# Experts as a chain of whole blocks with branch hints and one shared section for left-over tokens

## The chip, the cores and the metric

The kernel runs on one core of one Trainium2 chip. The metric is the device time of one execution in microseconds (us), as a median of runs. The engines are named as in the profile: PE (TensorE, matmuls; PEld its weight loads), DVE (VectorE), ACT (ScalarE), POOL (GpSimd) and SP (SyncE, which here only issues DMAs). Each engine has its own instruction stream, with its own copies of every branch; engines wait for each other by semaphores.

## The reference, cut to what matters

```python
x = attention(u, v, z)                 # (8*3072, 256) rows, squared-ReLU attention, times u
do_compute = x @ w_skip > 0            # about half of the rows
e_idx = argmax(x[do_compute] @ w_gate) # one of E = 8 experts for each such row
for e in range(8):                     # D = 256, F = 1024
    h = np.maximum(xc[mask] @ w1[e], 0.0)
    y[mask] = gate_w[mask, None] * (h @ w2[e])
out[do_compute] = xc + y
x = out
h = maximum(maximum(x @ m1, x @ m2), x @ m3)   # 256 -> 768, all 24576 rows
result = h @ m_out
```

How many rows an expert gets is known only on the chip. With the inputs that are timed, worked out from the reference, the eight experts get 1381, 1685, 1697, 1770, 1589, 1311, 1337 and 1665 rows.

## The kernel before

Everything is fp32, split into a high and a low part (float32r), and each product is three matmuls (high by high, low by high, high by low). The work has three stages: attention with routing, the experts, and the last layer (its three up-projections with a maximum, here called the max weights, and a down-projection).

Routing scatters each row, with its gate value and its row number, into a region of the DRAM tensor `xb` that belongs to its expert; skipped rows go straight to their place in the result part of `xb`. A table `tab` in SBUF holds the count of each expert and the row offset of each block of it. The last block's offset is set back so that a block of 512 never reaches beyond the expert's rows; rows that are computed twice give the same result twice.

An expert's rows are worked off in blocks of T = 512 rows. `block(e, s, k, o, side)` has eight steps f: `mm1` (L637 on) makes one 128-wide piece of the hidden layer with six matmuls of 512 columns into one of four PSUM buffers `ph`, ACT makes `h_hi` (L646) and DVE `h_lo` (L647); two steps later `mm2` (L651) multiplies that piece with w2, twelve matmuls of 256 columns into `y`. At the end `finish` (L663) lets DVE add the gated result to the rows `xr` (L667, one instruction for each 128 rows), and POOL scatters them (L90). `o` leaves out the first 0, 128 or 256 of the 512 rows, so the block's end comes in three sizes: 512, 384 and 256 rows. `k` picks the buffers `xr`, `ids` and half of `yb`. The dictionary `side` holds work that is written in front of a step: splitting the next expert's weights (`split_w`), transposing and splitting the next block's rows (`split_x`, from the raw rows `xq`), or loads on SP.

`body(e)` (L883) is the block that every expert is taken to have (block 0; of expert 0 block 1, since block 0 is done early, within the attention's end). It is straight code and carries most of the side work. `chain(e, n_e, j)` (L849) follows with tests at run time: is there a block j at all (L852), is it a full one (L863), and in the `Else` (L874) has it more than 256 rows. A full one calls `chain` for j + 1 inside itself, up to j = 6, where a loop takes over. So the code of the tails lies behind that of all deeper full blocks. With the counts above, expert 0 has body and a tail of 384 rows; experts 1, 2, 3, 4 and 7 have body, two full blocks and a tail of 256; experts 5 and 6 have body, one full block and a tail of 384.

At the end the order is another: the bodies of experts 6 and 7 follow each other, then come the chain of 6 and that of 7, with the first loads of the last layer between them (`load2`, `trans2`). The max weights and the down weights lie split in DRAM and are loaded in one go in the body of expert 1 (four DMAs of 1.5 MB).

The instruction order is written out by hand (`manual_schedule`), engine by engine in the order of the code. Where a branch joins, the framework brings the semaphores of both ways to the same count: the way that skips work waits for its own engine's last count and adds what the other way would have added.

Of the kernel before, what the change touches and what calls it, by code (L numbers as in the profile page):

```python
# [17 lines left out]
SP = mybir.EngineType.SP  # L18

# [7 lines left out]
def attention_moe_kernel(  # L27
# [43 lines left out]
    tab = const.tile([1, SNAP + 1], I32, name="tab")  # L71
# [63 lines left out]
    with ExitStack() as st:  # L135
# [459 lines left out]
        ids = [const.tile([P, TB, 1], I32, name=f"ids{k}") for k in range(2)]  # L595
# [9 lines left out]
        def load_x(src, q, n):  # L605
            why = "results go to rows before those of the experts"
            if q is not None:
                for i in load_blocks(nc.sync, xq[q], src[:, 0:D]):
                    tc.declare_no_dep(i, group="out", reason=why)
            if n is not None:  # L610
                i = nc.sync.dma_start(xr[n], src.rearrange("(n p) w -> p n w", p=P)).ins
                tc.declare_no_dep(i, group=f"out{1 - n}", reason=why)
# [9 lines left out]
        def split_x(q, s, h, eng=nc.vector):  # L622
            xt = xt1[0][:, h * T:(h + 1) * T]
            hi, lo = xT[s][0, h], xT[s][1, h]
            nc.vector.transpose(out=xt, in_=xq[q][h])
            split(hi, lo, xt, eng)
# [10 lines left out]
        def mm1(e, s, o, f, p):  # L637
            hi, lo = (t[:, o:] for t in hT[f % 4])
            c, p = f * P % T, p[:, o:]
            terms = [(h, i, m) for h in range(DH) for i, m in ((0, 0), (0, 1), (1, 0))]  # L640
            for k, (h, i, m) in enumerate(terms):
                nc.tensor.matmul(  # L642
                    p, e1[e % 2][i, h, f * P // T][:, c:c + P], xT[s][m, h][:, o:],
                    start=k == 0, stop=k == len(terms) - 1,
                )
# [5 lines left out]
        def mm2(e, k, o, f):  # L651
            b, hh = e2[e % 2][f], hT[f % 4]
            started = set()
            for n in range(o // P, TB):
                y, c = yb[2 * k + n // 2], slice(n * P, (n + 1) * P)
                for i, m in ((0, 0), (0, 1), (1, 0)):
                    nc.tensor.matmul(  # L657
                        y[:, n % 2], hh[i][:, c], b[:, m],
# [4 lines left out]
        def finish(k, o):  # L663
            x, ix = xr[k], ids[k]
            nc.vector.tensor_copy(ix, x[:, :, D + 1:D + 2])
            for n in range(o // P, TB):
                nc.vector.scalar_tensor_tensor(  # L667
                    x[:, n, 0:D], in0=yb[2 * k + n // 2][:, n % 2], scalar=x[:, n, D:D + 1], in1=x[:, n, 0:D],
                    op0=ALU.mult, op1=ALU.add,
                )  # L670
            scatter_rows(x, ix, range(o // P, TB), "out", f"out{k}")

        def block(e, s, k, o, side):
            for f in range(NF):
                for g in side.get(f, ()):
                    g()
                mm1(e, s, o, f, ph[f % len(ph)])
                if f > 1:
                    mm2(e, k, o, f - 2)
            for g in side.get(NF, ()):  # L680
                g()
            mm2(e, k, o, NF - 2)
            mm2(e, k, o, NF - 1)
            finish(k, o)
# [118 lines left out]
        block(0, 0, 0, 0, side)  # L803
        ph.append(bank_tile("pm", [P, T], "ph"))
        xt1.append(slab("ut", [P, DH * T], name="xt"))
        pieces = [slab(tag, dt=F32R, name="w") for tag in ("hh",) * 2 + ("ll",) * 2 + ("hl",) * 6]
# [5 lines left out]
        xT.append({(m, h): slab("a", dt=F32R, name="xT") for m in range(2) for h in range(DH)})  # L812
        for _ in weights:
            pass
# [8 lines left out]
        def spread(a):  # L823
# [7 lines left out]
        nc.vector.tensor_tensor(first, thr, spread(cnt), op=ALU.is_lt)  # L831
        nblk = r_p.tile([1, E], F32, name="nblk")
        nc.vector.tensor_reduce(nblk, first, axis=AX.X, op=ALU.add)
        nc.vector.tensor_copy(tab[:, E:2 * E], nblk)
        nc.vector.scalar_tensor_tensor(
            tab[:, SNAP:], in0=snap, scalar=float(2 * T), in1=cnt[:, 0:1], op0=ALU.is_ge, op1=ALU.mult
# [9 lines left out]
    def tokens_of(e):  # L846
        return nc.values_load(tab[0:1, e:e + 1], min_val=0, max_val=N)

    def chain(e, n_e, j, other=None):  # L849
        if j == NT:  # L850
            return
        with tc.If(n_e > j * T) as some:  # L852
            if j == NJ:
                n_b = nc.values_load(tab[0:1, E + e:E + e + 1], min_val=0, max_val=NT)
                with tc.For_i(NJ, n_b) as i:
                    with tc.manual_schedule():
# [3 lines left out]
                        block(e, 1, 0, 0, {})  # L860
                return
            s, k = 0 if (e, j) == (E - 1, 1) else 1 + (j - 1) % 2, j % 2
            with tc.If(n_e > j * T + 3 * P) as full:  # L863
                with tc.manual_schedule():
                    side = {}
                    if j + 1 < NJ:
                        src = source(e, j + 1)
                        load_x(src, 0, None)
                        load_x(src, None, 1 - k)
                        side = {5 + h: [do(split_x, 0, 1 + j % 2, h)] for h in range(DH)}  # L870
                    block(e, s, k, 0, side)
                chain(e, n_e, j + 1)
# [7 lines left out]
        if other is not None:  # L880
            with some.Else():
                other()
# [3 lines left out]
    def body(e):  # L886
        j0 = 1 if e == 0 else 0
        n_e = tokens_of(e) if e else None
        with tc.manual_schedule():
            side = {f: [] for f in range(NF + 1)}  # L890
            src = source(e, j0 + 1)
            load_x(src, 0, None)
            if e + 1 < E:
                if e != E - 2:
                    load_x(source(e + 1, 0), 1, None)
# [140 lines left out]
```

## Time and profile before

| | us |
|---|---|
| median of 3 runs (4335.49 to 4337.26) | 4336.86 |
| the profiled execution | 4339.29 |
| its span, first to last instruction | 4337.6 |
| PE busy in it | 4214.1 (97%) |
| experts, from the end of expert 0's body to the last layer's first matmul | 622.8 |

Times below are from the start of the span. A PE matmul's row is longer than the time until the next one starts, since they are pipelined: the pace is read from the distances between starts. "Idle before" is the time in which the engine did nothing before that instruction, and the arrow names what ended it; "issue" is an end that no semaphore explains. Branch instructions have no row of their own.

### The profile page before, as it was taken

To read this page: it belongs to the slowest core of one execution; us is meant where nothing else is said; L and a number is where in the kernel's file an instruction comes from. 1 tells how busy PE (TensorE), PEld (TensorE's weight loads), DVE (VectorE), ACT (ScalarE), POOL (GpSimd) and SP (SyncE) were. 2 spreads that over 40 slices of the span, in tenths; PEclk is the share of its full clock that TensorE was granted. 3 is DMA by queue.
4 is the path that set the end of the run, shared out by engine and by line. 5 is a ranking of instruction groups with operands and counts; after the bars stand their busy time and mean duration, and the time that the engine had idled before them with its cause. 6 is when DMAs were issued, how large, how long until landed. Compare 5 with 4: busy or idle time off the path is not lost.

```text
span 4337.6 us, 63208 instructions
## 1 busy us (share of the span) xinstructions
PE 4214.1 (97%) x22380; PEld 3609.0 (83%) x22380; DVE 2824.4 (65%) x5641; ACT 2160.0 (50%) x4048; POOL 403.8 (9%) x677
## 2 busy tenths in 40 slices
PE   7999999999999999999989899999999999999999
PEld 6888888888888888888888888888888888888887
DVE  6888888888888888887544454444444444444444
ACT  6777686877768687775322232222222222222222
POOL 2111110011111001003111112000000000000000
PEclk9999999999999999999999999999999999999999
DMA  7787868678786867877453432111111111111110
GB/s 191 188 200 188 188 184 195 175 197 196 192 186 181 206 178 194 197 187 171 129 135 86 94 93 66 33 30 35 34 30 30 32 37 30 30 30 40 30 30 25
DMA packets 849941, 506.30 MB, mean 117 GB/s; under 512 B 446850, under 2 KB 807810, under 8 KB 834146
## 3 DMA queue, kind: packets, MB, share of 16 engines
q1 hardware_dynamic: 832738, 455.58, 44.8%
q0 software_dynamic: 15712, 45.28, 3.2%
q8 instruction: 212, 3.47, 0.4%
q14 instruction: 223, 1.83, 0.1%
q10 hardware_dynamic: 1056, 0.13, 0.0%
HBM read 274.19 MB, written 202.03 MB: 110 GB/s over the span
## 4 chain that ended last, share of the span: by engine, by line
PE 89%; DMA 3%; DVE 2%; issue 2%; ACT 2%; SPq 1%; POOL 0%; DVEq 0%; ACTq 0%
PE ph L958 28%; PE acc L308 21%; PE acc L309 11%; PE ph L642 7%; PE y L657 6%; PE y L971 6%; PE s L241 3%; PE s L242 3%; PE y L972 3%; DMA xb<-xr,ids 1%; PE pm L354 1%; DVE alo L276 1%; DMA back<-mirror 1%; DMA vr<-in_v 1%; ACT ahi L275 1%
## 5 line engine op out<-in xcount | busy, mean ns | idle before, releaser
L308 PE MATMUL acc<-vt,ahi 128*128 128x512 f32 x4608 | 1649.6, 396 | 7.1 <-DVE x L325 3.3
L309 PE MATMUL acc<-vt,alo 128*128 128x256 f32 x4608 | 1292.6, 281 | 0.1
L958 PE MATMUL ph<-e,mw 128*128 128x512 f32 x5184 | 1249.9, 394 | 3.4 <-DMA xb<-xr,ids 3.4
L958 PEld LDWEIGHTS ph<-e,mw 128*128 128x128 f32 x5184 | 955.8, 188 | 219.2 <-issue 3.5
L308 PEld LDWEIGHTS acc<-vt,ahi 128*128 128x128 f32 x4608 | 868.4, 188 | 210.9 <-DVE x L325 4.9
L309 PEld LDWEIGHTS acc<-vt,alo 128*128 128x128 f32 x4608 | 872.8, 189 | 30.5 <-DVE alo L276 1.5
L619 ACT ACTIVATE h_hi<-r 128x512 fp32r<-128x512 f32 x288 | 182.0, 632 | 782.1 <-DVE r L963 782.1
L276 DVE TENSOR_TENSOR alo<-a,ahi 128x512 fp32r<-128x512 f32 x672 | 460.5, 685 | 147.2 <-ACT ahi L275 136.8
L247 ACT ACTIVATE a<-s 128x512 f32<-128x512 f32 x672 | 398.1, 592 | 192.2 <-PE s L242 169.4
L962 DVE TENSOR_TENSOR r<-ph,r 128x512 f32<-128x512 f32 x288 | 199.2, 692 | 376.2 <-PE ph L958 376.0
L275 ACT ACTIVATE ahi<-a 128x512 fp32r<-128x512 f32 x672 | 411.8, 618 | 11.1 <-DVE a L253 10.8
L971 PE MATMUL y<-mo,h_hi 128*128 128x512 f32 x1152 | 417.1, 394 | 0.0
L90 POOL DMA_INDIRECT xb<-x,idx x192 | 212.2, 1105 | 1752.1 <-DVE alo L276 1044.2
L276 DVE TENSOR_TENSOR alo<-back,ahi 128x512 fp32r<-128x512 f32 x480 | 329.9, 692 | 55.8 <-ACT ahi L275 46.1
L275 ACT ACTIVATE ahi<-back 128x512 fp32r<-128x512 f32 x480 | 289.0, 625 | 146.2 <-PE acc L308 96.4
L282 DVE STREAM_TRANSPOSE turned<-a 128x512 f32<-128x512 f32 x480 | 338.4, 705 | 13.3 <-DMA mirror<-turned 13.3
L620 DVE TENSOR_TENSOR h_lo<-r,h_hi 128x512 fp32r<-128x512 f32 x288 | 199.5, 693 | 201.1 <-ACT h_hi L619 201.1
L647 DVE SCALAR_TENSOR_TENSOR h_lo<-ph,h_hi 128x512 fp32r<-128x512 f32 (+2 forms) x232 | 146.3, 631 | 276.5 <-ACT h_hi L646 264.7
L972 PE MATMUL y<-mo,h_lo 128*128 128x256 f32 x1152 | 325.4, 282 | 0.2 <-DVE h_lo L620 0.2
L963 DVE TENSOR_TENSOR r<-ph,r 128x512 f32<-128x512 f32 x288 | 199.2, 692 | 182.0 <-PE ph L958 182.0
L646 ACT ACTIVATE h_hi<-ph 128x512 fp32r<-128x512 f32 (+2 forms) x232 | 127.5, 549 | 378.7 <-PE ph L642 341.1
L241 PE MATMUL s<-hh,hl 128*128 128x512 f32 x672 | 271.8, 405 | 36.4 <-ACT a L247 22.4
(129 smaller groups left out, 4984.3 us busy)
## 6 DMA issues: line engine op xcount, KB each, us to landing
mirror<-turned SPq DMA_DIRECT2D x120, 1024.0 KB
back<-mirror SPq DMA_DIRECT2D x480, 256.0 KB
xq<-xb SPq DMA_DIRECT2D x608, 64.0 KB
vr<-in_v SPq DMA_DIRECT2D x48, 512.0 KB
ut<-in_u SPq DMA_DIRECT2D x48, 512.0 KB
out<-r SPq DMA_DIRECT2D x47, 512.0 KB
r<-in_moe_w SPq DMA_DIRECT2D x16, 1024.0 KB
xr<-xb SPq DMA_DIRECT2D x29, 528.0 KB
```

What stands on the lines that cost most here:

```text
L241: nc.tensor.matmul(s, w, hh, start=True, stop=False)
L247: nc.scalar.activation(a, s, AF.Relu)
L275: nc.scalar.activation(hi, a, AF.Copy)
L276: nc.vector.tensor_tensor(lo, a, hi.bitcast(F32), op=ALU.subtract)
L282: nc.vector.transpose(out=turned[0][:, :, n], in_=a.rearrange("k (c j) -> k c j", j=Q))
L308: nc.tensor.matmul(o, hn, vv, start=kb == 0, stop=False, skip_group_check=True)
L309: nc.tensor.matmul(o[:, 0], ln, vv[:, 0], start=False, stop=kb == KB - 1, skip_group_check=True)
L642: nc.tensor.matmul(p, e1[e % 2][i, h, f * P // T][:, c:c + P], xT[s][m, h][:, o:], start=k == 0, stop=k == len(terms) - 1,)
L657: nc.tensor.matmul(y[:, n % 2], hh[i][:, c], b[:, m], start=f == 0 and n // 2 not in started, stop=f == NF - 1 and i == 1, skip_group_chec ...
L958: nc.tensor.matmul(p, w[:, h, s, c], xT2(i, m, h), start=k == 0, stop=k == len(terms) - 1)
L971: nc.tensor.matmul(yb[n], hh[0][:, c], mo[:, f], start=f == 0, stop=False, skip_group_check=True)
L972: nc.tensor.matmul(yb[n][:, 0], hh[1][:, c], mo[:, f, 0], start=False, stop=f == NFF - 1, skip_group_check=True)
```

## The change

1. `chain` keeps only whole blocks: one test for each block, whether more than 384 rows of it are there, no `Else`. A full block hints the branch of the next one at step 3.
2. What is left over (at most 384 rows) is worked off after the chain in `rest`: a block of the last 256 rows, and if more than 256 are left a second one of 128 rows (`first=1, end=2`). It has buffers of its own: `xr` and `ids` number 2, the split rows `xT[3]`, raw rows `xq[2]` over the router weights `wgs`; the results use the `yb` of k = 0, swapped (`result`).
3. These rows (384 of them) are loaded at the end of the expert before, and split in the body at steps 1 and 2. For expert 0 they are loaded and split in its own body, at steps 6 and 7, and the weight splits there move to earlier steps.
4. Hints: `foresee` writes on all five engines an instruction that computes the branch's condition and hands it to the instruction fetch as a hint for a named branch.
5. Six small DVE operations make the left-over counts; `body` loads two numbers of the table in place of one.
6. Experts 6 and 7 now come in the same order as the others; `trans2` stands between expert 7's chain and its `rest`.
7. The max weights are loaded in four parts, at the ends of the bodies of experts 1 to 4.

```diff
-        def mm1(e, s, o, f, p):
+        def mm1(e, s, cols, f, p):
...
+        def result(k, n):
+            return yb[(2 * k + n // 2) if k < 2 else 1 - n // 2], n % 2
...
-        def block(e, s, k, o, side):
+        def block(e, s, k, side, first=0, end=TB):
+            ns, cols = range(first, end), slice(first * P, end * P)
...
+        spare = wgs.bitcast(F32).rearrange("p c q e -> p (c q e)")
+        xq.append([spare[:, h * T:(h + 1) * T] for h in range(DH)])
+        xr.append(slab("x", name="xr"))
...
+    def foresee(label, taken):
+        tc.mark_branch_hint_location(label, hint=taken, engines=ENGINES)
...
-    def chain(e, n_e, j, other=None):
-        if j == NT:
-            return
-        with tc.If(n_e > j * T) as some:
+    def chain(e, n_e, j):
+        with tc.If(n_e > j * T + 3 * P, label=label("full", e, j)):
...
-            with full.Else():
-                with tc.If(n_e > j * T + 2 * P) as most:
-                    with tc.manual_schedule():
-                        block(e, s, k, P, {})
-                with most.Else():
-                    with tc.manual_schedule():
-                        block(e, s, k, 2 * P, {})
+            k = j % 2
+            with tc.manual_schedule():
+                side = {3: [do(foresee, label("full", e, j + 1), n_e > (j + 1) * T + 3 * P)]}
+                if j + 1 < NJ:
+                    src = source(e, j + 1)
+                    load_x(src, 0, None)
+                    load_x(src, None, 1 - k)
+                    side |= {5 + h: [do(split_x, 0, 1 + j % 2, h)] for h in range(DH)}
+                block(e, 1 + (j - 1) % 2, k, side)
+            chain(e, n_e, j + 1)
+
+    def rest(e, n_r, then=()):
+        with tc.If(n_r > 0):
+            with tc.manual_schedule():
+                block(e, 3, 2, {1: [do(foresee, label("more", e), n_r > 2 * P)]}, first=2)
+            with tc.If(n_r > 2 * P, label=label("more", e)):
+                with tc.manual_schedule():
+                    block(e, 3, 2, {1: then}, first=1, end=2)
...
+            else:
+                load_x(source(e, NT - 1), 2, None, P)
             if e + 1 < E:
-                load_x(src, None, 1 - j0)
+                load_x(source(e + 1, 0), 1, None)
+                for f, k in zip((0, 1, 2, 2, 3, 3, 4, 5) if e == 0 else (1, 2, 3, 4, 4, 5, 6, 7), range(8)):
+                    side[f].append(do(split_w, e + 1, k))
+            load_x(src, None, 1 - j0)
+            load_x(source(e, NT - 1), None, 2, P)
             for h in range(DH):
+                side[5 + h].append(do(split_x, 0, 1 + j0, h))
+                side[(6 if e == 0 else 1) + h].append(do(split_x, 2, 3, h, P))
...
+            if 0 < e < 5:
+                side[NF].append(do(load_m, e - 1))
+            side[6 if e == 0 else 3].append(
+                lambda: foresee(label("full", e, j0 + 1), regs[0] > (j0 + 1) * T + 3 * P)
+            )
+            block(e, j0, j0, side)
```

Three places show how the instructions stand. First PE at the tail of expert 1 (`w` are its weights). Before, this is the part behind the `Else` of block 3: a jump leads to it past the code of the deeper blocks, a second one to its 256-row form.

```order
L874 COMPARE_AND_BRANCH
L642 MATMUL ph<-xT,w 128x384 x18
L657 MATMUL y<-w,h_hi 128x256 [waits Activation_49]
L657 MATMUL y<-w,h_hi 128x256
...
L874 UNCONDITIONAL_BRANCH [waits PE_sequencer_49]
L642 MATMUL ph<-xT,w 128x256 x18
L657 MATMUL y<-w,h_hi 128x256 [waits Activation_49]
```

Now the same tail stands behind the joins of the six tests (after a test that fails, one of the six rows with the waits is run):

```order
L883 UNCONDITIONAL_BRANCH [waits PE_49,PE_sequencer_49] x6
L871 TENSOR_LOAD tab
L905 COMPARE_AND_BRANCH
L646 MATMUL ph<-xT,w 128x256 [waits DVE_49]
L646 MATMUL ph<-xT,w 128x256 x5
L874 REGISTER_ALU
L1077 BRANCH_PREFETCH_HINT
L646 MATMUL ph<-xT,w 128x256 [waits DVE_49]
```

The first matmul of the tail had no wait; now PE waits for its own last matmul, loads a number of the table and then waits for DVE's count.

DVE has the same joins at that place, here of expert 1 (`h_lo` of the rest's steps follows, then its results):

```order
L883 UNCONDITIONAL_BRANCH [waits DVE_49,DVE_sequencer_49] x6
L871 TENSOR_LOAD tab
L905 COMPARE_AND_BRANCH
L651 SCALAR_TENSOR_TENSOR h_lo<-ph,h_hi 128x256 [waits Activation_49]
L874 REGISTER_ALU
L1077 BRANCH_PREFETCH_HINT
L651 SCALAR_TENSOR_TENSOR h_lo<-ph,h_hi 128x256 [waits Activation_49] x7
```

DVE_49 is the count that PE's first matmul waits for; DVE raises it there after its own last instruction of the block before.

The third place is DVE in the body of expert 0, steps 5 to 7. Before (`xq` are the two halves of one load, the rows of the tail; `w` are weights):

```order
L625 STREAM_TRANSPOSE xt<-xq 128x512 [waits DMAHW5_49,DMAHW6_49,DMAHW4_49,DMAHW3_49]
L620 TENSOR_TENSOR xT<-xt,xT 128x512 [waits Activation_49]
L647 SCALAR_TENSOR_TENSOR h_lo<-ph,h_hi 128x512 [waits Activation_49]
L620 TENSOR_TENSOR w<-r_24766,w 128x256 [waits Activation_49] x2
L625 STREAM_TRANSPOSE xt<-xq 128x512 [waits DMAHW2_49,DMAHW7_49,DMAHW1_49,DMAHW0_49]
L620 TENSOR_TENSOR xT<-xt,xT 128x512 [waits Activation_49]
L917 TENSOR_LOAD tab [waits DVE_49]
L647 SCALAR_TENSOR_TENSOR h_lo<-ph,h_hi 128x512 [waits Activation_49]
```

Now (`wgs` are the rows of the left-over section):

```order
L629 STREAM_TRANSPOSE xt<-xq 128x512 [waits DMAHW5_49,DMAHW6_49,DMAHW4_49,DMAHW3_49]
L624 TENSOR_TENSOR xT<-xt,xT 128x512 [waits Activation_49]
L651 SCALAR_TENSOR_TENSOR h_lo<-ph,h_hi 128x512 [waits Activation_49]
L871 TENSOR_LOAD tab [waits DVE_49] x2
L629 STREAM_TRANSPOSE xt<-wgs 128x384 [waits DMAHW5_49,DMAHW4_49,DMAHW6_49,DMAHW3_49,DVE_49]
L624 TENSOR_TENSOR xT<-xt,xT 128x384 [waits Activation_49]
L629 STREAM_TRANSPOSE xt<-xq 128x512 [waits DMAHW2_49,DMAHW7_49,DMAHW1_49,DMAHW0_49]
L624 TENSOR_TENSOR xT<-xt,xT 128x512 [waits Activation_49]
L874 REGISTER_ALU
L1077 BRANCH_PREFETCH_HINT
L651 SCALAR_TENSOR_TENSOR h_lo<-ph,h_hi 128x512 [waits Activation_49]
```

In front of step 6's `h_lo` there is now a transpose that waits for a load of its own, which SP issues after the eight DMAs of the first load; the load of expert 1's rows, which is split at the body's end, is issued behind it. The weight splits are gone from there, to earlier steps.

## Rows read from the trace of the kernel before

**Rows 1.** The page, parts 1 (busy time) and 4 (chain).
```profile
PE 4214.1 (97%) x22380; PEld 3609.0 (83%) x22380; DVE 2824.4 (65%) x5641; ACT 2160.0 (50%) x4048; POOL 403.8 (9%) x677
...
PE 89%; DMA 3%; DVE 2%; issue 2%; ACT 2%; SPq 1%; POOL 0%; DVEq 0%; ACTq 0%
```

**Rows 2.** Windows from tail to tail: span, busy by engine, PEclk, DMA share, GB/s.
```profile
2102.48:2131.69 29.21, 20.41 (x122) 19.81 (x121) 8.94 (x20) 4.57 (x9) 5.72 (x10) 0.82 0.51 120
2131.69:2226.84 95.15, 83.15 (x528) 76.28 (x529) 41.36 (x78) 26.78 (x52) 15.59 (x27) 0.93 0.54 157
...
sum 622.82, PE 561.87 PEld 518.24 DVE 275.18 ACT 176.63 POOL 110.94; mean PE 80.27 PEld 74.03 DVE 39.31 ACT 25.23 POOL 15.85
```

**Rows 3.** Waits of PE, 2102 to 2726: total, times, longest.
```profile
PE ph L642 <- issue: 53.2, 15, 9.5
PE ph L958 <- DMA xb<-xr,ids: 3.4, 1, 3.4
PE ph L642 <- ACT e L619: 2.6, 1, 2.6
PE ph L642 <- DVE xr L667: 1.8, 1, 1.8
```

**Rows 4.** Timeline of PE: start, time, instructions, idle before and its end.
```profile
2131.69 5.98 PE L642 MATMUL ph<-xT,w 128*128 128x512 f32 x18 [1.82 <-DVE xr L667]
...
2210.60 4.21 PE L642 MATMUL ph<-xT,w 128*128 128x256 f32 x18 [9.49 <-issue]
2226.84 4.35 PE L642 MATMUL ph<-xT,e 128*128 128x512 f32 x18 [2.51 <-issue]
2299.66 4.21 PE L642 MATMUL ph<-xT,e 128*128 128x256 f32 x18 [5.02 <-issue]
2547.26 3.41 PE L642 MATMUL ph<-xT,w 128*128 128x384 f32 x18 [1.94 <-issue]
```

**Rows 5.** Timeline of PE, steps of 384 rows and of 512.
```profile
2116.98 1.21 PE L642 MATMUL ph<-xT,e 128*128 128x384 f32 x6
2119.09 1.21 PE L642 MATMUL ph<-xT,e 128*128 128x384 f32 x6
...
2138.93 1.55 PE L642 MATMUL ph<-xT,w 128*128 128x512 f32 x6
2141.76 1.55 PE L642 MATMUL ph<-xT,w 128*128 128x512 f32 x6
```

**Rows 6.** Timeline of DVE at expert 1's last full block and its tail.
```profile
2200.44 1.66 DVE L667 SCALAR_TENSOR_TENSOR xr<-y,xr 128x256 f32<-128x256 f32 x4 [2.14 <-PE y L657]
...
2219.75 0.42 DVE L647 SCALAR_TENSOR_TENSOR h_lo<-ph,h_hi 128x256 fp32r<-128x256 f32 x1 [1.02 <-ACT h_hi L646]
2221.19 0.42 DVE L647 SCALAR_TENSOR_TENSOR h_lo<-ph,h_hi 128x256 fp32r<-128x256 f32 x1 [1.01 <-ACT h_hi L646]
...
2224.37 0.88 DVE L667 SCALAR_TENSOR_TENSOR xr<-y,xr 128x256 f32<-128x256 f32 x2 [1.24 <-PE y L657]
```

**Rows 7.** Windows: the gap before expert 1's tail, and four us behind it.
```profile
2201.11:2210.60 9.49, 0.00 (x1) 0.00 (x0) 0.99 (x3) 0.00 (x0) 4.17 (x7) 0.70 0.88 324
2210.60:2214.60 4.00, 4.00 (x18) 4.00 (x19) 0.85 (x2) 0.77 (x2) 0.00 (x0) 0.50 0.05 8
```

**Rows 8.** DMA issues between 2131 and 2227: count and size.
```profile
mw<-mwd SPq DMA_DIRECT2D x3, 1536.0 KB
```

**Rows 9.** Waits of DVE, 2102 to 2725.
```profile
DVE h_lo L647 <- issue: 9.7, 7, 3.0
```

**Rows 10.** Tile xq in the body of expert 0: durations, first and last start.
```profile
L105 SPq DMA_DIRECT2D xq<-xb x16: 3/436/697, 2088.6 to 2097.1; - x16
```

**Rows 11.** Timeline of DVE in the body of expert 0.
```profile
2093.21 0.71 DVE L625 STREAM_TRANSPOSE xt<-xq 128x512 f32<-128x512 f32 x1 [1.47 <-DMA xq<-xb]
2094.62 0.69 DVE L620 TENSOR_TENSOR xT<-xt,xT 128x512 fp32r<-128x512 f32 x1 [0.70 <-ACT xT L619]
```

**Rows 12.** Timeline of PE in the body of expert 0, step 7.
```profile
2096.62 1.55 PE L642 MATMUL ph<-xT,e 128*128 128x512 f32 x6
```

More of the change, by code (lines that the diff above doesn't have):

```diff
@@ L594, in attention_moe_kernel @@
         e1, e2 = [[]], [[]]
-        ids = [const.tile([P, TB, 1], I32, name=f"ids{k}") for k in range(2)]
+        ids = [const.tile([P, TB, 1], I32, name=f"ids{k}") for k in range(3)]
         def source(e, j):
@@ L620, in split, with split_x @@
             eng.tensor_tensor(lo, src, hi.bitcast(F32), op=ALU.subtract)
[L622 to L626, printed above, removed]
+        def split_x(q, s, h, o=0):
+            xt = xt1[0][:, h * T + o:(h + 1) * T]
+            hi, lo = xT[s][0, h][:, o:], xT[s][1, h][:, o:]
+            nc.vector.transpose(out=xt, in_=xq[q][h][:, o:])
+            split(hi, lo, xt)
         def split_w(e, i, raw2=None, eng=nc.vector):
@@ L802, in attention_moe_kernel @@
         side[NF] = [settle]
-        block(0, 0, 0, 0, side)
+        block(0, 0, 0, side)
         ph.append(bank_tile("pm", [P, T], "ph"))
         xt1.append(slab("ut", [P, DH * T], name="xt"))
-        pieces = [slab(tag, dt=F32R, name="w") for tag in ("hh",) * 2 + ("ll",) * 2 + ("hl",) * 6]
+        pieces = [slab(tag, dt=F32R, name="w") for tag in ("ll",) * 2 + ("hl",) * 6]
         for _ in range(2):
@@ L859, in chain @@
                             split_x(0, 1, h)
-                        block(e, 1, 0, 0, {})
+                        block(e, 1, 0, {})
                 return
-            s, k = 0 if (e, j) == (E - 1, 1) else 1 + (j - 1) % 2, j % 2
-            with tc.If(n_e > j * T + 3 * P) as full:
-                with tc.manual_schedule():
[L865 to L872, printed above, removed]
-            with full.Else():
-                with tc.If(n_e > j * T + 2 * P) as most:
-                    with tc.manual_schedule():
-                        block(e, s, k, P, {})
-                with most.Else():
-                    with tc.manual_schedule():
-                        block(e, s, k, 2 * P, {})
-        if other is not None:
-            with some.Else():
-                other()
+            k = j % 2
[13 more added lines that the diff above has]
+            with tc.If(n_r > 2 * P, label=label("more", e)):
+                with tc.manual_schedule():
+                    block(e, 3, 2, {1: then}, first=1, end=2)
     regs = []
@@ L887, in body @@
         j0 = 1 if e == 0 else 0
-        n_e = tokens_of(e) if e else None
+        if e:
+            regs[:] = [number(e), number(TAIL + 1 + e)]
         with tc.manual_schedule():
             side = {f: [] for f in range(NF + 1)}
+            if e == 0:
+                side[6].append(lambda: regs.extend((number(SNAP), number(TAIL))))
             src = source(e, j0 + 1)
             load_x(src, 0, None)
-            if e + 1 < E:
-                if e != E - 2:
-                    load_x(source(e + 1, 0), 1, None)
-                for k in range(8):
-                    side[(1, 2, 3, 4, 4, 5, 6, 7)[k]].append(do(split_w, e + 1, k))
@@ L926, in again @@
                     split_x(0, 1, h)
-                block(0, 1, 1, 0, {})
-        chain(0, tokens_of(0), 2)
-    chain(0, body(0), 2, again)
-    for e in range(1, E - 2):
-        chain(e, body(e), 1)
-    n_y, n_z = body(E - 2), body(E - 1)
+                block(0, 1, 1, {})
+        chain(0, number(0), 2)
+        rest(0, number(TAIL + 1))
+        passes[0] = 0
+    for e in range(E):
+        n_e, n_r = body(e)
+        if e == E - 1:
+            break
+        chain(e, n_e, 2 if e == 0 else 1)
+        if e:
+            rest(e, n_r)
+            continue
+        rest(e, n_r, [do(foresee, "again", n_e < 1)])
+        with tc.If(n_e < 1, label="again"):
+            again()
     hs = {}
```

100 lines of the change are left out of this document (56 added, 44 removed).

## The prediction

> **What bounds the kernel now.** I read the page's busy times and chain first: PE is busy 97% of the span and 89% of the chain, all else is small [rows 1]. So a change counts where it removes PE time or PE idling. The windows from tail to tail cut out the stage that is edited: the experts, from the end of expert 0's body to the last layer's first matmul, take 622.8 us, with PE busy in 561.9 of them and its clock below full, 0.82 in the stretch of expert 0 [rows 2]. The waits of PE show what the idling is: 61.0 us in 18 waits, of which 53.2 in 15 end with "issue", no semaphore [rows 3]. The timeline puts them at the branches: 9.49 and 5.02 us before tails of 256 rows, 1.94 before one of 384, 2.51 from a tail to the next body [rows 4]. The one that comes from full block to full block has none. So the price is that of a jump to code far away; 256-row tails take two jumps and pay about twice.
>
> How much of the stage is work? A step of a full block takes 2.83 us (2138.93 to 2141.76), one of a 384-row tail 2.11 (2116.98 to 2119.09) [rows 5]; one of a 256-row tail 1.44, read from DVE, which follows PE there (2219.75 to 2221.19) [rows 6], twelve matmuls of 0.12 us. With eight steps a block has 22.6, 16.9 or 11.5 us. The stage holds 19 full blocks, five tails of 256 and three of 384 rows: 429 + 58 + 51 = 538 us. Lost are 622.8 - 538 = 85 us: the 61 of waits and 24 in which PE ran slowly behind them. The latter shows at expert 1: in the four us after the 9.49 us gap the clock is 0.50, the lower of its two levels, 1.2 GHz [rows 7], and 18 matmuls of 256 columns take 4.21 us [rows 4] in place of 18 x 0.12 = 2.2.
>
> **The change part by part.**
>
> *The work itself.* Full blocks stay 19. The tails become eight of 256 rows, 8 x 11.5 = 92 us, and three pieces of 128 rows (experts 0, 5, 6). A step of such a piece has six matmuls of 128 columns and three of 256. The trace has no fp32r matmul of 128 columns: between half of 0.12 us and all of it, a step costs 0.72 to 1.08 us and a piece 5.8 to 8.6. I take 8.6, since the row it is nearest to is the 256-column pace, and each matmul still loads 128 weight columns: 26 us for three. In all 429 + 92 + 26 = 547 us, 9 more than before. The Trainium skill, TensorE: Matmul & The Clock Gate, section LDWEIGHTS (loading the stationary operand), bears on this: a weight load takes as long as its columns at 1.2 GHz, 107 ns for 128, and fp32 has no faster load. By that rule 128 columns are bound by the load, and the pieces cost 8 us more than by half the pace; no run here shows such a matmul alone.
>
> *The jumps.* Before, PE had 8 jumps into an Else, 5 more into its 256-row half and 8 back. Now it has, per expert, one jump past the blocks that are not there, and for the five small tails one past the 128-row piece; expert 0 adds one past its second pass. All of them are hinted a block or seven steps ahead, so I take the fetch as done in time and the 53 us of issue as gone. What is late next? The order shows it: the first matmul of the left-over block waits for DVE's count at the join, which DVE raises after its last result. DVE finishes 0.99 us after PE's last matmul of a full block (2200.44 + 1.66 = 2202.10 against 2201.11) [rows 6, 7], 0.92 after a 256-row tail (2225.25 against 2224.33, the gap's start) [rows 4, 6]. From there to PE's first matmul I add 0.4 us: the gap of 1.82 us that a DVE row released [rows 3] is such a handover with three results. PE's own wait for its last matmul and its load of one number run beside this. So 8 x 1.4 after full blocks, 5 x 1.3 after small tails (the last of them into the last layer), 3 x 0.9 after 128-row pieces (one result in place of two), 1.2 for the second-pass test and the last layer's longer list of waits: 21.6 us. Bounds: zero, if PE runs ahead as from full block to full block, and 32 (a 2.0 us gap at 16 places, as after the 384-row entries today).
>
> *The clock behind them.* Today 24 us go with 61 us of gaps. Of the short gaps, that of 1.94 us was followed by full speed (18 matmuls of 384 columns in 3.41 us), that of 1.82 by 5.98 us for 18 of 512 columns, where two steps at full speed need 4.3 [rows 4]. I take 5 us; bounds 0 and 27 (1.7 at each of 16).
>
> *Expert 0's body.* Its left-over rows are loaded and split inside it. SP issues 16 row loads from 2088.6 to 2097.1, one per 0.5 us, and the first transpose waits 1.47 us for its four and starts at 2093.21 [rows 10, 11]. The new eight DMAs take the place of the second load; the half that step 6 needs lands at about 2098, as the second load's issue times plus the 2.5 us of the first suggest. Behind it on DVE stand two transposes and two splits, with ACT's copies 0.7 us each in between [rows 11], about 3.7 us in all, and then step 6's h_lo. That ends near 2102.4; PE wants it three us earlier, one full-block step after step 7 began at 2096.62 [rows 12]. Step 7 queues likewise, and expert 1's load lands last, so DVE's results of this body end some 3 us late as well, and PE's left-over block waits for them. I take 6 us for both; bounds 0 (the splits of weights have left these steps) and 10.
>
> *What costs nothing.* The 384-column splits of the other experts stand at steps 1 and 2 of the body, where DVE has 2.83 us a step and 0.69 + 0.68 + 1.1 us of work; a last full block still splits rows that nobody uses, as today's splits those of the tail. Hints are two short instructions on each engine, under PE's queue; if they were not covered and each took 0.1 us, the 29 that run would make 3. I put 3 us in for this and for code behind a jump's target that is not yet there. The four max weight loads cost PE today what lies in the 9.49 us gap over the 5.02 of its neighbours: DMA was 88% busy at 324 GB/s in it [rows 7], three 1.5 MB loads and a fourth were under way [rows 8]. That goes with the jump. trans2 now has only the last tail's 13 us to end in; I price it at nothing because it starts before that tail does, up to 2 if POOL is held by its scatters.
>
> *Sum.* 547 + 21.6 + 5 + 6 + 3 = 582.6 against 622.8: 40.2 us less. The profiled execution took 4339.3, 2.4 over the median of the runs, so 4339.3 - 40.2 - 2.4 = 4296.7: I predict **4297 us**.
>
> **The rivals.**
>
> *The hints bring nothing.* Then each far jump still waits for code. PE's entries with one jump cost 1.94 us today, but DVE jumps as well: it sat up to 3.0 us on "issue" at such places [rows 9], and now PE waits for DVE. 3.3 us after 8 full blocks, 3.0 at 5 small tails, 0.9 at 3 pieces, 4 for the rest make 48 us of gaps; with 24/61 of a us of slow clock for each, 19; 547 + 48 + 19 + 6 + 3 = 623: 4337 us, no change. For it: no hint is run in the trace of before, so nothing there shows that one works. The Trainium skill, Runtime: NRT & Kernel Launch, section Instruction fetch mechanics, speaks for it: code is fetched ahead in sequence only, and a taken branch outside the fetched pages stalls; it knows of no hint. The trace agrees on today's jumps (53.2 us of issue).
>
> *The hints do harm.* One mechanism: the code fetched by a hint takes the place of the code that comes next in line, and PE runs dry once in the block that carries the hint. Place: the middle of bodies, full blocks and left-over blocks, 29 hints that run. Price: the 2.51 us of today's short gap and 1.0 of slow clock. From twelve such stalls on it outweighs the 40 us; with all 29 the time is 4297 + 102 = about 4400. Against it: a block is worth 20 us, so a late fetch has room to hide.
>
> *PE runs ahead.* If the joins do not hold PE (DVE's count is there early) and 128 columns run at half the pace, 20 us of gaps, 5 of clock and 8 of weight loads go too: 4264 to 4275.
>
> **How the numbers follow.** Forecast 0.64, with a range of its own of 4280 to 4318; hints bring nothing 0.16; hints harm 0.07; PE runs ahead 0.13. 0.2% of 4337 is 8.7 us, about what a measurement can tell from no change: faster means under 4328. The forecast and the last rival are faster (0.77), of the no-hint case a quarter (0.04); it is the same with half (0.08) and a little of the forecast's upper end; slower with a quarter of it and the harm. Faster 0.81, same 0.10, slower 0.09. The range of 8 in 10 goes from 4270 to 4329: it leaves out most of the no-hint case, the harm, and the far end of the last.
>
> **What would show it.** In the new profile PE's issue waits should fall from 53 us to under 10, and its waits at the left-over block's L646 should name DVE's results with 1 to 2 us each. The gap before expert 1's tail should be no longer than its neighbours. The stage should take 575 to 600 us. Expert 0's body should show PE waiting for h_lo at step 6 or 7. The steps of 128-row pieces should show as 0.7 to 1.1 us. I am wrong if issue stays above 30 us (no hint), if issue waits turn up inside blocks (harm), or if the gaps at joins are far from 1.4.

## The result, and the profile after

The changed kernel takes 4298.78 us, median of 4 runs (4297.26 to 4300.71), against 4337.06 (4335.49 to 4342.35) before: a ratio of 0.991, with a 95% interval from 0.9893 to 0.9927. That is 38.3 us less. The prediction said 4297, in a range from 4270 to 4329. The profiled execution took 4298.98 us, its span is 4297.2.

PE's share on the page, for [rows 1], went from 97% to 98%:

```profile
PE 4211.3 (98%) x22524; PEld 3610.6 (84%) x22524; DVE 2844.6 (66%) x5707; ACT 2168.3 (50%) x4088; POOL 403.8 (9%) x674
```

The windows, cut at the same places as in [rows 2] (columns: span, then busy PE, PEld, DVE, ACT, POOL, then PEclk, DMA share, GB/s), first the experts' stretch before, then the changed kernel with attention ahead of the experts and the last layer behind them:

```profile
2102.48:2725.30 622.82, 561.87 (x3577) 518.24 (x3577) 275.18 (x520) 176.63 (x341) 110.94 (x180) 0.95 0.38 98
```

```profile
0.00:2100.60 2100.60, 2046.26 (x11316) 1764.30 (x11316) 1767.11 (x3889) 1527.12 (x2847) 292.30 (x497) 0.99 0.74 187
2100.60:2682.12 581.52, 555.23 (x3721) 514.07 (x3720) 292.07 (x574) 184.62 (x379) 108.93 (x175) 0.99 0.46 116
2682.12:4297.20 1615.08, 1609.76 (x7488) 1332.21 (x7488) 785.42 (x1244) 456.57 (x863) 2.60 (x3) 1.00 0.16 32
```

The experts take 581.5 us, 41.3 less than in [rows 2]; 582.6 were predicted. PE is idle for 26.3 of them, not 61, and its clock is 0.99, not 0.95. The other two parts moved by a few us: attention ends 1.9 earlier (in all runs below it ends somewhere from 2099.9 to 2108, so that is mostly noise, and the experts' stretch in the traces tells kernels apart better than the total does), and the last layer is 2.8 longer.

PE's waits between 2100 and 2684 (total, times, longest), which answer to [rows 3]:

```profile
PE ph L646 <- DVEq L883: 15.6, 8, 4.1
PE ph L646 <- DVEq L908: 4.5, 4, 1.1
PE ph L646 <- DVEq L978: 3.3, 1, 3.3
PE ph L1004 <- ACT e L623: 3.0, 1, 3.0
PE ph L1004 <- POOL e L624: 0.9, 1, 0.9
```

Not one wait ends with "issue" any more, where [rows 3] had 53.2 us of them. What ends them is a semaphore of DVE's instruction stream ("DVEq") at the three kinds of joins: L883 behind the chain, L908 behind the left-over block, L978 behind the second-pass test of expert 0. DVE's own issue waits, 9.7 us in [rows 9], are nearly gone as well:

```profile
DVE h_lo L651 <- issue: 0.6, 2, 0.3
```

The single gaps are in PE's timeline (start, time, instructions, idle before and its end), to be held against [rows 4]:

```profile
2095.28 0.51 PE L665 MATMUL y<-e,h_hi 128*128 128x256 f32 x2 [1.49 <-ACT h_hi L650]
2104.70 4.21 PE L646 MATMUL ph<-xT,e 128*128 128x256 f32 x18 [4.10 <-DVEq L883]
2130.44 2.11 PE L646 MATMUL ph<-xT,w 128*128 128x512 f32 x5 [3.27 <-DVEq L978]
2200.97 2.42 PE L646 MATMUL ph<-xT,w 128*128 128x256 f32 x18 [1.12 <-DVEq L883]
2213.86 4.33 PE L646 MATMUL ph<-xT,e 128*128 128x512 f32 x18 [1.12 <-DVEq L908]
2284.56 3.87 PE L646 MATMUL ph<-xT,e 128*128 128x256 f32 x18 [2.92 <-DVEq L883]
2577.03 3.23 PE L646 MATMUL ph<-xT,e 128*128 128x256 f32 x17 [2.93 <-DVEq L883]
2682.12 0.50 PE L1004 MATMUL ph<-e,mw 128*128 128x512 f32 x1 [2.95 <-ACT e L623]
```

Expert 1's tail (2200.97), which waited 9.49 us in [rows 4], now waits 1.12, and its 18 matmuls of 256 columns run at full speed (2.42 us, not 4.21). Nine of the joins have 1.12 to 1.18. Four stand out: 4.10 at expert 0, 3.27 at its second-pass test, and 2.92 and 2.93 at experts 2 and 6. Behind the gap of 2.92 the clock is down, behind that of 1.18 us before expert 7's tail it is not (windows of four us each):

```profile
2284.56:2288.56 4.00, 4.00 (x21) 4.00 (x22) 0.85 (x2) 0.81 (x3) 1.76 (x3) 0.59 0.80 176
2667.40:2671.40 4.00, 4.00 (x33) 4.00 (x34) 1.27 (x3) 1.21 (x4) 3.14 (x5) 1.00 0.32 108
```

Why expert 0's is the longest stands in DVE's timeline at the end of its body, for [rows 11]: the split of expert 1's rows ends at 2102.9, and only then come the results for which PE has been waiting since 2100.6.

```profile
2100.79 0.71 DVE L629 STREAM_TRANSPOSE xt<-xq 128x512 f32<-128x512 f32 x1 [0.40 <-DMA xq<-xb]
2102.25 0.69 DVE L624 TENSOR_TENSOR xT<-xt,xT 128x512 fp32r<-128x512 f32 x1 [0.76 <-ACTq L883]
...
2102.93 1.65 DVE L676 SCALAR_TENSOR_TENSOR xr<-y,xr 128x256 f32<-128x256 f32 x4
```

The pieces of 128 rows, which no row of before could show, in PE's timeline of expert 5:

```profile
2520.50 2.12 PE L646 MATMUL ph<-xT,w 128*128 128x128 f32 x18
...
2523.90 0.78 PE L646 MATMUL ph<-xT,w 128*128 128x128 f32 x6
...
2524.93 0.78 PE L646 MATMUL ph<-xT,w 128*128 128x128 f32 x6
```

A step takes 1.03 us and the piece 8.3. Less three matmuls of 256 columns at 0.12 us, the six of 128 columns take 0.11 us each: half the columns save less than a tenth. That is the pace of the weight load which the prediction took from the Trainium skill (TensorE: Matmul & The Clock Gate, section LDWEIGHTS (loading the stationary operand)): 107 ns for 128 columns. The trace agrees, with its 0.11 us.

### The profile page after: what moved, and what is told of

Its sections match the earlier page's. It is cut to its first block, busy times and chain, and to the rows that moved or that the text cites. A ratio compares the mean times of both kernels' runs of the same rounds, so it can differ in the third digit from the quotient of the medians.

```text
span 4297.2 us, 64384 instructions
## 1 busy us (share of the span) xinstructions
PE 4211.3 (98%) x22524; PEld 3610.6 (84%) x22524; DVE 2844.6 (66%) x5707; ACT 2168.3 (50%) x4088; POOL 403.8 (9%) x674
## 5 line engine op out<-in xcount | busy, mean ns | idle before, releaser
L1004 PE MATMUL ph<-e,mw 128*128 128x512 f32 x5184 | 1252.0, 395 | 3.9 <-ACT e L623 3.0
L1004 PEld LDWEIGHTS ph<-e,mw 128*128 128x128 f32 x5184 | 957.8, 189 | 219.6 <-ACT e L623 3.2
L252 ACT ACTIVATE a<-a 128x512 f32<-128x512 f32 x465 | 294.3, 633 | 14.8
L1007 ACT ACTIVATE r<-ph 128x512 f32<-128x512 f32 x288 | 170.7, 593 | 240.6 <-PE ph L1004 240.6
```

The lines of the kernel that those rows point to most:

```text
L252: nc.scalar.activation(a, a, AF.Square)
L1004: nc.tensor.matmul(p, w[:, h, s, c], xT2(i, m, h), start=k == 0, stop=k == len(terms) - 1)
```

## The experiments

**Are the hints the cause?** Four kernels that differ from the changed one in `foresee` alone.

```diff
     def foresee(label, taken):
-        tc.mark_branch_hint_location(label, hint=taken, engines=ENGINES)
+        pass
```

> The changed kernel with no hints of its own; all else stays (chains of whole blocks, shared section, loads). Theory (the hints take the jumps' code fetch off the path): the waits at the joins grow from 1.1 us to 3 to 5 us at the 13 to 16 places, with slow clock behind them, and the time goes back to 4325 to 4345 us, near the 4337 of before. Rival (the new layout does it, one short jump in place of two long ones): within 5 us of the changed kernel, 4295 to 4304 us.

Measured: 4317.45 us (4315.07 to 4317.94), ratio to before 0.9951 (0.9934 to 0.9967). That is midway: neither the theory nor its rival. Its gaps on PE:

```profile
2206.78 3.63 PE L646 MATMUL ph<-xT,w 128*128 128x256 f32 x18 [2.31 <-PEq L871]
2221.16 4.33 PE L646 MATMUL ph<-xT,e 128*128 128x512 f32 x18 [1.12 <-DVEq L908]
2291.57 0.61 PE L646 MATMUL ph<-xT,e 128*128 128x256 f32 x3 [2.64 <-PEq L871]
```

The entry into a 256-row tail costs 2.3 to 2.7 us here at experts 1 to 7, ended by PE's own stream (PEq), where [rows 4] had 5.02 (two more waits, of 2.37 and 1.88 us, end with "issue" inside the tails of experts 0 and 4); and the way from the tail into the next body costs 1.12 with no hint at all, where [rows 4] had 2.51. So the change without its hints takes off half. The reading is that this is the layout: one far jump in place of two, and none on the way out, since the next body now lies right behind the left-over section. The experts' stretch tells the sizes:

```profile
2100.40:2701.26 600.86, 563.55 (x3720) 521.74 (x3720) 292.46 (x575) 184.56 (x379) 109.01 (x175) 0.97 0.45 112
```

From 622.8 to 600.9 by the layout (the four parts of the max weights with it), from there to 581.5 by the hints: 19.3 us, of which 8.3 are PE's busy time (563.55 against 555.23, the slow clock behind longer gaps) and 11 the gaps themselves. Of the first step, PE's idle time gives 23.6 us: 14.9 at the entries into the tails of experts 1 to 7, of which 7.2 at expert 1 alone (9.49 to 2.31), and 8.5 at the ways out of the tails. No run separates the jumps from the loads of the max weights, so how much of the 7.2 belongs to which is not shown.

```diff
-        tc.mark_branch_hint_location(label, hint=taken, engines=ENGINES)
+        tc.mark_branch_hint_location(label, hint=taken, engines=ENGINES[:1])   # PE alone
```

> Hints on PE alone. Theory (PE waits at a join for DVE's count, so DVE's jump must be fetched ahead too): PE's waits at the joins name DVE's sequencer with 2.5 to 3.5 us each in place of 1.1, and the time is 4315 to 4335 us. Rival (only PE's own jumps matter): 4297 to 4303 us.

Measured: 4296.03 us (4295.0 to 4299.94), ratio 0.9902 (0.9886 to 0.9919): the same as with hints on all five engines. My theory fell, the rival held. With `ENGINES[1:]`, all but PE:

> Hints on ACT, DVE, POOL and SP, none on PE. Theory (PE's own jump is the longer fetch): PE's waits at the joins are 3 to 6 us, and the time is 4320 to 4345 us. Rival (PE's own fetch hides beside DVE's last results, about 1 us): under 4310 us.

Measured: 4320.01 us (4315.09 to 4322.34), ratio 0.9956 (0.994 to 0.9973): the same as with no hints. All of the 19 us belongs to PE's hints. PE's first waits in the run without PE's hints, and in the run with PE's alone:

```profile
PE ph L646 <- PEq L871: 16.1, 5, 5.2
PE ph L646 <- DVEq L883: 9.7, 3, 3.8
```

```profile
PE ph L646 <- DVEq L883: 15.2, 7, 4.4
PE ph L646 <- DVEq L908: 4.5, 4, 1.1
PE ph L646 <- DVEq L978: 3.3, 1, 3.3
```

The second list is nearly that of the changed kernel, the 3.3 us at L978 included: nothing here shows that DVE's hints make DVE's jumps any faster.

The last of the four moves the hints of PE and all others from step 3 (of the left-over block from step 1) to the end of their block (`NF`).

> All hints kept but moved to the end of their block, some 3 us of PE work before the jump, in place of 14 us (step 3) in full blocks. Theory (a fetch takes 2 to 3 us): just in time, 4297 to 4306 us. Rival (a fetch takes 5 us or more, as the 5.0 us gaps of before suggest): 2 to 3 us at 13 joins come back, 4320 to 4340 us. If the two gaps of 2.9 us (experts 2 and 6) come from code fetched in line between the hint and the jump, they fall to 1.1 us here.

Measured: 4299.12 us (4298.04 to 4300.31), ratio 0.9911 (0.9895 to 0.9928), the experts 581.4 us. A hint some 3 us ahead of the jump is as good as one 14 us ahead. The 2.93 us at experts 2 and 6 stayed, so they do not come from code fetched between hint and jump.

**What are the 2.9 us at experts 2 and 6?**

```diff
                 block(0, 1, 1, {})
+            for _ in range(64):
+                nc.vector.memset(pad, 0.0)
```

> 64 memsets on DVE added in the branch for expert 0's second pass, which does not run: DVE's code of experts 1 to 7 lies 64 instructions further on, nothing else differs. Theory (the two joins of 2.9 us are DVE's fetch, set by where its code lies): the long joins are no longer at experts 2 and 6, but at others or at none; the time stays within 5 us, 4293 to 4303 us. Rival (they belong to the work of experts 2 and 6): 2.9 us at the same two.

Measured: 4303.11 us (one run, at the upper end of what was expected), the experts 578.1 us. The joins of experts 2 and 6 have 1.12, and expert 5's is now the long one (its lines count one higher):

```profile
2290.02 2.17 PE L647 MATMUL ph<-xT,e 128*128 128x256 f32 x16 [1.12 <-DVEq L884]
2514.74 3.65 PE L647 MATMUL ph<-xT,w 128*128 128x256 f32 x18 [2.96 <-DVEq L884]
2582.30 2.41 PE L647 MATMUL ph<-xT,e 128*128 128x256 f32 x18 [1.12 <-DVEq L884]
```

The shift is one run, but the two places are no chance of a run: in the hints-late kernel above and in the two kernels with the max weights in one go and with `trans2` moved (both below), where DVE's code up to there is as long as in the changed kernel, the long joins are those of experts 2 and 6 again. So which join is long is set by where DVE's code lies. With PE's hints alone, where DVE's code is shorter, the long ones were at experts 5 and 6 (3.04 and 3.20).

**What are the 1.12 us at the others?** The prediction took them for DVE's last results.

```diff
-            for n in ns:
+            for n in ns[:2] if lean[0] and len(ns) == TB else ns:
                 y, m = result(k, n)
```

> DVE's last two of the four results (rows 256 to 511) are left out in every full block and body, so part of the output is missing; DVE is then done with a block 0.2 us behind PE's last matmul in place of 1.0. Theory (two things run side by side at a join and both take about 1.05 us: DVE's results, and PE's own chain of two semaphore steps, a jump, a load of one number and a test): the gaps after full blocks stay at 1.0 to 1.1 us. Rival (DVE's results alone hold PE): 0.4 to 0.7 us.

The other kernel has this and

```diff
-        if e:
-            regs[:] = [number(e), number(TAIL + 1 + e)]
         with tc.manual_schedule():
+            if e:
+                regs[:] = [number(e), number(TAIL + 1 + e)]
```

> As the run before (same results left out), and the two numbers of an expert are loaded at the start of its body, so that PE's chain at the join has no load. Theory: both sides are shorter now, the gaps after full blocks fall to 0.6 to 0.7 us. Rival (DVE's results alone hold PE): the same 0.4 to 0.7 us as in the run before.

Measured at expert 1's tail, in the first and in the second:

```profile
2204.89 2.41 PE L646 MATMUL ph<-xT,w 128*128 128x256 f32 x18 [1.12 <-PEq L873]
```

```profile
2202.31 2.41 PE L646 MATMUL ph<-xT,w 128*128 128x256 f32 x18 [0.72 <-DVEq L885]
```

With shorter results the gap stays at 1.12 (five of seven joins, 1.12 to 1.19; the other two, of experts 6 and 7, have 2.23 and 2.24 and end with DVE) and only its end changes its name, to PE's own stream, with the load of the number at L873. With the load gone too it is 0.70 to 0.77 at seven. The load alone does not move it either: in the combined version below, which has all results and the early loads, the same joins have 1.09 to 1.10, but for the long two. Two things of equal length run side by side there. (The loads turn up elsewhere: the entries into bodies went from 1.12 us to between 1.35 and 1.48, and behind 128-row pieces from none to 0.7.)

**Do the four parts of the max weights matter?**

```diff
-            if 0 < e < 5:
-                side[NF].append(do(load_m, e - 1))
+            if e == 1:
+                for k in range(4):
+                    load_m(k)
```

> The changed kernel with the max weights loaded in one go in the body of expert 1, as before. Theory (the long gap of 9.49 us before expert 1's tail was a code fetch behind these loads; a hint 14 us ahead of the jump leaves it time): expert 1's join stays within 1 us of the 1.12 us of the others, and the time within 4 us of the changed kernel's, 4295 to 4303 us. Rival (the fetch waits behind the loads, hint or not): 3 to 8 us at expert 1's join with slow clock behind it, 4303 to 4312 us.

Measured: 4312.96 us (4308.06 to 4315.89), ratio 0.994 (0.9925 to 0.9955). Expert 1's join has 1.12, but that does not test the theory. Here SP issues all four loads from 2147.6 to 2149.5, and ahead of the join the DMA is all but idle; in the kernel before, SP issued two of them in the body and the other two only at 2192, shortly ahead of the gap of 9.49 us that began at 2201.11 (first three lines of before, then a window of this run that ends where its join begins):

```profile
2136.98 0.96 SPq L910 DMA_DIRECT2D mw<-mwd  x2
2191.89 0.39 SPq L910 DMA_DIRECT2D mw<-mwd  x1
2192.33 0.46 SPq L911 DMA_DIRECT2D mo<-mod  x1
```

```profile
2200.00:2211.82 11.82, 11.82 (x83) 10.86 (x81) 5.86 (x11) 3.06 (x5) 0.00 (x0) 1.00 0.02 4
```

Whether a hint covers a jump while such loads run stays open. The time is near the rival's, by a way that neither named. PE and DVE in the first full block of expert 1, the loads of `wgs` that stand on SP ahead of the rows for the block after it (issue times in ns: shortest, median, longest), and the window ahead of the wait:

```profile
2182.86 0.80 PE L665 MATMUL y<-w,h_hi 128*128 128x256 f32 x2 [5.83 <-ACT h_hi L650]
```

```profile
2180.95 0.71 DVE L629 STREAM_TRANSPOSE xt<-xq 128x512 f32<-128x512 f32 x1 [11.02 <-DMA xq<-xb]
```

```profile
L107 SPq DMA_DIRECT2D wgs<-xb x8: 320/988/6286, 2158.8 to 2172.3; - x8
```

```profile
2148.00:2170.00 22.00, 22.00 (x143) 20.09 (x142) 13.63 (x26) 8.31 (x16) 0.00 (x0) 1.00 1.02 388
```

The six MB, and two of expert weights behind them, fill the DMA (share 1.02, 388 GB/s). One issue on SP takes up to 6.29 us, so SP comes to the next block's rows only at 2176.4 (2160.1 in the changed kernel, whose experts begin 4.2 us earlier). DVE waits 11.02 us for them, and PE 5.83 for what ACT and DVE make behind that. The experts take 591.95 us, 10.4 more: 5.9 of idle time and 4.5 of busy time, at a clock of 0.97 in place of 0.99.

**Can the rest be had?** First the last layer's entry.

```diff
     chain(E - 1, n_e, 1)
-    with tc.manual_schedule():
-        for h in range(DH):
-            trans2(0, h, nc.gpsimd)
-    rest(E - 1, n_r)
+    rest(E - 1, n_r, (), {2 + 2 * h: [do(trans2, 0, h)] for h in range(DH)})
```

Here `rest` puts this work into its 256-row block, and into an `Else` where there is none.

> The transposes and splits for the last layer's first block moved into expert 7's left-over block (steps 2 and 4), where the text of the change had them ahead of it; in its instruction order they stand behind it. Theory: the last layer's first matmuls lose their waits of 2.95 and 0.94 us and some of the slow clock behind them, 4 to 7 us less: 4291 to 4295 us. Rival (DVE and ACT have no room in steps of 1.44 us): PE waits 2 to 4 us inside that block instead, 4296 to 4300 us.

Measured: 4298.52 us (4296.08 to 4299.78), ratio 0.9909 (0.9894 to 0.9924), no difference in the time. In the trace the waits of 2.95 and 0.94 became one of 1.25, and the last layer is 1612.3 us as before the change; the experts are 0.7 longer. So the edit does what it says, for about 2 us in place of the 4 to 7 expected, too few to be told by the runs. The rival's time came, but not its waits: no wait inside that block is in the trace.

Then 384 left-over rows in one block (`first=1`), with a test of its own:

> Left-over rows over 256 (experts 0, 5, 6) as one block of 384 rows in place of 256 and 128; the test for it is hinted too, at step 7. Theory (128-column matmuls are bound by their weight loads): three times 11.5 + 9.0 - 16.9 = 3.6 us less, 10.8, and about 3 back for the join behind a 384-row block, so 7 to 10 us less: 4288 to 4292 us. Rival (a second hint displaces the first): PE's joins wait 2.3 to 2.7 us again at up to 8 places, 4305 to 4315 us.

Measured: 4304.05 us (4300.88 to 4306.67), ratio 0.9923 (0.9909 to 0.9936). A little under the rival's price, and not at its places. The experts' stretch is 583.5 us, 2.0 longer than in the changed kernel: PE is busy for 7.6 us less (547.6) and idle for 9.6 more. Experts 5 and 6 gained some 2 us each, but expert 0 lost more at the two ends of its left-over block:

```profile
2111.72 5.66 PE L646 MATMUL ph<-xT,e 128*128 128x384 f32 x18 [8.86 <-PEq L907]
2136.89 6.11 PE L646 MATMUL ph<-xT,w 128*128 128x512 f32 x18 [5.72 <-DVEq L982]
```

At expert 0 two hinted jumps in a row on PE took 8.86 us, where the one of the changed kernel took 4.10. But experts 5 and 6 take the same two jumps, with waits of 1.84 and 3.26 us, so two hints in a row do not explain it by themselves. Whether the second hint displaced the first was not tried alone.

Last, a version of all that helped: `trans2` as above, the numbers loaded early, and expert 1's rows split in expert 0's left-over block in place of the end of expert 0's body.

```diff
-                if e + 1 < E:
+                if 0 < e < E - 1:
                     side[NF].append(do(split_x, 1, 0, h))
...
-        rest(e, n_r, [do(foresee, "again", n_e < 1)])
+        rest(e, n_r, [do(foresee, "again", n_e < 1)], {2 + 2 * h: [do(split_x, 1, 0, h)] for h in range(DH)})
```

> The changed kernel with three edits: the last layer's first transposes in expert 7's left-over block; the splits of expert 1's rows in expert 0's left-over block in place of the end of its body; the numbers loaded at the start of each body. Theory (DVE's results of expert 0's body stand behind those splits, 4.10 us gap): the gap there falls to 1.2 to 2.2 us; with the last layer's waits gone and a little clock, 4290 to 4295 us. Rival (the gap at expert 0 is DVE's fetch of code, not the splits): it stays at 3 to 4 us, and the time is 4295 to 4299 us.

Measured: 4294.99 us (4294.37 to 4297.56), ratio 0.9898 (0.9882 to 0.9915). It beats the kernel before by 1.0%; against the changed kernel the 3.8 us lie within what a measurement can tell. In the traces the experts take 1.5 us less than there (580.0) and the last layer 2.9 less. Expert 0's gap fell from 4.10 to 1.09, with one more of 0.77 inside the block behind it, so most of it was DVE's splits, not its code:

```profile
2101.64 1.58 PE L646 MATMUL ph<-xT,e 128*128 128x256 f32 x11 [1.09 <-DVEq L883]
```

The same with one block of 384 rows for experts 5 and 6:

> As the combined version, and experts 5 and 6 work their left-over rows as one block of 384 rows; expert 0 keeps 256 and 128. Theory: 2 us less for each of the two (in the run with 384-row blocks the stretch from expert 5's join to the next body was 18.9 against 20.7 us, and 21.9 against 24.3 for expert 6): 4286 to 4292 us. Rival (the added test and its hint cost as much): the same as the combined version within 2 us.

Measured: 4300.41 us (4294.56 to 4303.07), ratio 0.9904 (0.9888 to 0.9921). No gain, by neither of the two expectations; the experts' stretch is 584.8 us, 4.7 longer than in the combined version. The joins of experts 1 and 2 ended with PE's own stream again, at 1.89 and 2.30 us, those of 3 and 4 at 1.10 as before, though the blocks of all four carry two hints; those of experts 6 and 7 have 3.16 and 3.22. What makes the difference stays open.

## Why the prediction was right, step by step

- *The work, 547 us.* Right. 19 blocks of 22.6, eight tails of 11.6 (2508.89 to 2520.50) and three pieces of 8.3 in place of 8.6 make 547.
- *The joins, 21.6 us.* Too high. The waits at L646 are 23.4 us and the one at L1004 2.95 more, but 3.0 of that belong to expert 0's body, 5.8 to DVE's jumps and 1.8 to `trans2` (all below). What is left are 14 joins of 1.12, 15.7 us: full blocks and small tails alike have 1.12 (1.4 and 1.3 predicted), and behind the 128-row pieces of experts 5 and 6 there is none (0.9 predicted). The reason given was half of it: PE's own wait and load, which "run beside this", are as long as DVE's results, and it takes both edits to move the gap.
- *The clock, 5 us.* Too low: 555.2 of busy time against 547 of work is 8.2. (The 18 matmuls that the prediction compares with "two steps" of 4.3 us are those of three steps; the 4.3 is right.)
- *Expert 0's body, 6 us.* Right in kind: 1.8 us of stalls for the piece of step 6 (1.49 until ACT's `h_hi`, which stands behind the copies of the splits, and 0.34 until DVE's `h_lo`), which lie ahead of the experts' stretch, and 3.0 over the other joins at its end, 4.8 in all. The combined version shows that the splits on DVE were the cause of the second. The first is not the same in all traces: 1.41 to 1.57 us in the changed kernel and the four hint runs, 2.85 to 3.51 in the eight runs made later; why stays open.
- *Hints and code, 3 us.* Too low: DVE's jumps cost 2 x 1.8 at experts 2 and 6 and 2.15 at the second-pass test over the other joins, 5.8. The hints themselves cost nothing that the traces show.
- *"What costs nothing".* The max weights: expert 1's join has 1.12 as said, but its long gap had another course than the prediction read from [rows 8]. Two of the four loads were issued 64 us ahead of the gap; under way in it were the third and the fourth (2191.9 and 2192.3) and 2 MB of expert weights behind them. Whether they or the jump made its excess is not shown. That the four parts have a worth of their own was not foreseen: with the rows of the left-over section ahead on SP, one go costs 10 us. `trans2`: wrong. It was priced at nothing "because it starts before that tail does". Its two transposes stand behind the left-over section's join on DVE (in the trace they start at 2680.70, released by the join at L908), which the order of the changed program would have told; PE waits 2.95 and 0.94 us, and the last layer is 2.8 us longer (1614.8 to 1616.0 us in the ten kernels with `trans2` there, 1612.2 to 1612.3 in the three that moved it).
- *The sum, 582.6 against 581.5 us.* The terms measured are 547 + 15.7 + 8.2 + 3.0 + 5.8 + 1.8. The joins were 5.9 too high and expert 0's body 3.0 (within the stretch); the clock was 3.2 too low, DVE's jumps 2.8 and `trans2` 1.8. That these cancel to 1.1 us is luck. What was not luck is the main step: the waits with "issue" went from 53.2 us to none, and joins of 1.1 us took their place.
- *The rival "the hints bring nothing", 4337.* It did not happen, but its price was wrong by 20 us, as the run without hints shows (4317). It took 3.0 us for each exit from a small tail (1.12 measured) and 3.3 for each entry (2.3 to 2.7), that is, it gave the layout no credit. Its price for one jump had a counterexample in the trace of before: expert 0's tail of 384 rows, with one jump, had waits of 4.79 and 2.19 us, not 1.94. The forecast put the whole gain down to hints; of the 41 us in the experts, 22 came with the rest of the change (by the gaps, the second jump, the way out and expert 1's long gap) and 19 by PE's hints. The total came out because both are in the change.
- *The rival "the hints do harm"* found nothing in the changed kernel: none of its waits in the experts ends with issue. *"PE runs ahead"* holds only behind the 128-row pieces.

## What to carry to other kernels

Where a wait ends with "issue" behind a branch, count the far jumps on the way first, and lay the code so that the common path falls through; then hint the jump that is left, and find out by runs with the hints of one engine at a time which of them count (here PE's alone). At a join, write down everything that each engine does there, PE's own loads and tests too: to shorten one of two equal chains moves nothing (1.12 us with DVE's shortened, 1.10 with PE's). And look up in the instruction order where each moved piece came to stand, also those that one prices at nothing (`trans2` cost 2.8 us of the last layer).

## What the runs showed of the hardware

- A hint on PE for a far jump brought gaps of 2.3 to 2.7 us down to the 1.12 us that the join takes anyway, and 3 us ahead is early enough (581.4 us for the experts, against 581.5 with 14 us).
- On DVE it saves nothing that shows: L978 has 3.27 with and 3.28 us without. Its jump to the left-over section costs 1.8 to 2.1 us extra at some places of its code and nothing at others, and 64 instructions ahead of them change which.
- Behind gaps of 1.1 us PE ran on at its upper level (18 matmuls of 256 columns in 2.41 to 2.42 us); behind gaps of 2.3 us and more it mostly spent part of them at the lower one, 1.2 GHz (3.2 to 4.2 us for the same), though not always (2.41 us behind 2.30 without hints, 2.42 behind 2.95 without PE's, 2.41 behind 3.20 with PE's alone).
- With eight MB of loads issued just before, one 48 KB DMA issue on SP took up to 6.29 us, in place of 0.32 to 0.86 for the same loads in the changed kernel.
